# Keys and queries of the next batch loaded half a batch sooner and transposed by DMA in the middle FFN1; first unit with four query tiles and its sampled copies on GpSimd

## The chip, the cores and the metric

The kernel runs on one core of a Trainium2 chip. The metric is the device time of one launch in microseconds (us), the median of several runs; lower is better.

## The reference

Block-sparse attention with 4 batches, 8 heads, 768 tokens, head size 64, followed by a feed-forward network over 3072 tokens of width 512 with 2048 hidden units. Tokens are in 24 blocks of 32.

```python
scores = (1.0 / np.sqrt(D)) * np.matmul(q, k.transpose(0, 1, 3, 2))
mask = np.abs(blk_i - blk_j) <= 1
mask = mask | (blk_i == 0) | (blk_j == 0) | (blk_i == n_blocks - 1) | (blk_j == n_blocks - 1)
for qb in range(n_blocks):
    for kb in sampled_blocks[qb]:            # 3 random blocks for each query block
        mask[qb * 32:(qb + 1) * 32, kb * 32:(kb + 1) * 32] = True
scores = np.where(mask, scores, -1e9)
attn = np.exp(scores - scores.max(-1, keepdims=True))
attn = attn / (attn.sum(-1, keepdims=True) + 1e-09)
x = np.matmul(attn, v)                       # heads put side by side: 3072 x 512
h = x @ w_in
out = (0.5 * h * (1.0 + erf(h / sqrt(2)))) @ w_out
```

Query blocks 0 and 23 see all keys (the dense blocks). Every other block sees 8 blocks: the first, its own three, three sampled ones and the last.

## The kernel before

**Units.** The work is cut into nine units, each some quads (four query blocks, 128 tokens) of one batch: unit 0 is quad 1 of batch 0 and that batch's dense blocks; unit 1 quads 0 and 2; unit 2 quads 3 to 5; then for each of batches 1 to 3 a unit with quads 0 to 2 and the dense blocks (units 3, 5, 7) and one with quads 3 to 5 (units 4, 6, 8). The program alternates: FFN1 of unit n (eight steps of two hidden tiles, `ffn1_step`, Gelu on ScalarE into `g`), then the attention of unit n+1 with FFN2 of unit n (`ffn2_pieces`) filled in between in the amounts of a list of quotas, written by hand.

**Attention.** A unit is a list of rounds: `d` rounds for the dense blocks (one end `x`, one head group `G`), `s` rounds for two sparse blocks. Iteration `it` issues the scores of round it+1 (PE, `sc`), the division of a finished group (`den`, `rec`, `xh` on VectorE), the 32x32 transposes of round it-1 (`pT` or `ptd`, VectorE), the maxima of round it+1 (`nm`, VectorE), the exponentials of round it (`pp`, ScalarE), then hooks, the FFN2 fill, and the values of a group that is complete (`av`, PE). There is one buffer of `av` (psV) and two of scores (psA). Every engine works through its own queue in the program's order.

**Gathered keys and values.** `gb` holds for each sparse query block its eight key blocks. `gather_fixed` (lines 249 to 256, VectorE) copies the blocks whose place is known; `gather` (line 265) copies the sampled ones, one copy for each, at a block number that `block_numbers` has loaded into registers of VectorE or of GpSimd (POOL). For the second unit and part of the third, GpSimd makes the sampled copies.

**Batch 0.** Keys and queries come in with heads side by side (`load_kq`), PE transposes them (`turn_heads`) and ScalarE puts them in place (`place_heads`), keys in `k0`, which lies in the space of `qT1`; line 614 later copies `k0` whole to `kvs[0]`. The value loads (`load_v`, eight) and then the weights (`load_w_in`, `load_w_out`, four each) are issued from GpSimd's queue.

**Batches 1 to 3.** `load_by_token` loads keys and queries in six parts each (line 111, GpSimd's queue), held back by `hold_loads`, a one-element copy that waits for a slice of `g`. `turn` (lines 117 and 118) transposes both by DMA on SP's queue, keys into the space of `ptd`. `place_keys` (line 122, VectorE) scales the keys into `kvs`. Before, the loads for batch b+1 stand in FFN1 of the middle unit (1, 3, 5), `turn` at hook 2 of the attention of units 2, 4 and 6, `place_keys` at the start of the FFN1 of units 2, 4 and 6, just ahead of the gathers, and the value loads there too (batch 1: in FFN1 of unit 0).

Of the kernel before, what the change touches and what calls it, by code (L numbers as in the profile page):

```python
# [19 lines left out]
def kernel(  # L20
# [99 lines left out]
    def place_keys(b):  # L120
        for pr in range(NPR):
            nc.vector.tensor_scalar_mul(
                keys(b)[:, 0:NB, BL * pr:BL * pr + BL].rearrange("p (c n) k -> p c n k", c=NC),
                kTd.rearrange("p (c r n k) -> p r c n k", c=NC, r=NPR, k=BL)[:, pr], 1.0 / 8.0)

# [94 lines left out]
    def place_heads(which, pr, pt):  # L220
        if which == "k":
            nc.scalar.mul(k0[:, 0:NB, BL * pr:BL * pr + BL].rearrange("q n (a i) -> q n a i", i=PI),
                          pt.rearrange("q i (n a) -> q n a i", n=NB), 1.0 / 8.0)
        else:
            nc.scalar.copy(qT0[:, :, pr, :].rearrange("q c (p i) -> q c p i", i=PI),
                           pt.rearrange("q i (c p) -> q c p i", c=NC))

    def spaces():

        views = [psT.tile([P, PI, PP], BF16, name="pt", tag="T")]  # L230
        two = psV.tile([P, 2, 1024], BF16, name="pq", tag="V")
        views += [two[:, i, 0:S].rearrange("p (i c) -> p i c", i=PI) for i in range(2)]
        return views + [psO.tile([P, PI, PP], BF16, name="pt", tag="op")]
# [35 lines left out]
    class Unit:  # L269
        def __init__(self, b, quads, dense, i0=0):  # L270
# [4 lines left out]
            self.rounds = [("d", x, G) for x in (0, 1) for G in (0, 1)] if dense else []  # L275
# [288 lines left out]
    first = [psA.tile([P, 2, 1024], BF16, name="pk", tag="A") for _ in range(2)]  # L564
    first = [x[:, i, 0:S].rearrange("p (i c) -> p i c", i=PI) for x in first for i in range(2)]
    first += spaces()
    for i, (which, pr) in enumerate([(w, pr) for w in "kq" for pr in range(NPR)]):
        turn_heads(which, pr, first[i])
        place_heads(which, pr, first[i])
    spare_key(k0)  # L570
    gather(units[0], units[0].js, known, 0, KC)
    gather_fixed(k0, units[0].place)
    for part in range(4):
        load_w_in(part)
    for part in range(4):
        load_w_out(part)
    others = block_numbers(J0[7:], POOL)
    gather(units[1], J0[7:], others, 0, KC, nc.gpsimd)

    def second_values():  # L580

        nc.gpsimd.tensor_copy(mark, sampled(units[0].place[units[0].js[-1]], NR - 1)[0:1, BW - 1:BW])
        gather(units[1], J0[7:], others, KC, BW, nc.gpsimd)
        ones(1)
    attention(units[0], iter(()), [0] * 7, (0, 0, 0), 5,
              {4: [lambda: gather(units[0], units[0].js, known, KC, BW)], 5: [second_values]})

    QUOTAS = {0: ([4, 3, 1, 1, 0], (1, 2, 1)), 1: ([6, 5, 5, 3, 3, 1, 1], (2, 2, 1))}
    for n, unit in enumerate(units):
# [17 lines left out]
        for s in range(KOUT // 2):  # L607
            ffn1_step(n, 2 * s)
            if s == 0:
                if n == 0:  # L610
                    hold_loads(0)
                    for h in range(H):
                        load_v(1, h)
                    nc.gpsimd.tensor_copy(kvs[0][:, :, 0:KC], k0)
                    gather(units[2], J1[7:], block_numbers(J1[7:], POOL), engine=nc.gpsimd)
                if n > 0 and not fresh and b + 1 < B:
                    hold_loads(0)
                    load_by_token(kn, k, b + 1)
                    load_by_token(qn, q, b + 1)
                if fresh and b + 2 < B:  # L620
                    hold_loads(0)
                    for h in range(H):
                        load_v(b + 2, h)
                if fresh:
                    others = block_numbers(J0[7:], DVE)
            if s == 7 and nxt is not None:
                table(AF.Exp)
            if fresh and s == 0:
                place_keys(b + 1)
                spare_key(keys(b + 1))  # L630
# [6 lines left out]
        elif n in QUOTAS:  # L637
            attention(nxt, filler, *QUOTAS[n],
                      hooks={2: [lambda: turn(1)]} if n == 1 else None)
        elif fresh:  # L640
            attention(nxt, filler, [6, 6, 4, 0, 6, 6, 4, 0, 2, 2, 1], (2, 3, 3), late=True)
        else:
            attention(nxt, filler, [8, 8, 5, 5, 6, 2, 1], (2, 3, 5),
                      hooks={2: [lambda: turn(b + 1)]} if b + 1 < B else None)
# [30 lines left out]
```

## Time and profile before

| | |
|---|---|
| median of 3 runs | 319.88 us (319.59 to 321.11) |
| the profiled execution | 320.74 us, its span 319.0 us |
| mean granted TensorE clock | 0.979 |
| busy, of the span | PE 268.3 us (84%), DVE 218.5 (68%), ACT 208.4 (65%), POOL 88.7 (28%) |
| FFN1 of units 0, 1 and 2 start at | 33.88, 56.52 and 84.48 us |
| FFN1 of units 3 to 8 start at | 122.36, 155.71, 192.99, 225.41, 262.75 and 293.98 us |

Times in the views count from the span's start. In lines of the timeline and of the chain the first two numbers are start and duration in us; then come the engine, the line of the kernel, the operation, what it writes and what it reads, how many, and in brackets the idle time ahead of it with what ended it. "issue" there is time in which the engine waited for nothing that the profile shows. PEld is TensorE's weight load, SPq the issuing queue of SyncE. In the view by stages each row has the stage, its length, and busy time and number of instructions for each engine, then the granted clock, the DMA share and GB/s.

### The profile page before, as it was taken

How to read it: one execution, taken by the hardware profiler on the slowest of the kernel's cores; microseconds unless marked ns; L12 is line 12 of the kernel's file. 1: busy time of each engine (PE TensorE's matmuls, PEld its weight loads, DVE VectorE, ACT ScalarE, POOL GpSimd, SP SyncE). 2: the span in 40 equal slices, each digit the busy share in tenths (PEclk: the TensorE clock that was granted, in tenths of full speed). 3: DMA queues.
4: the chain of work that ended last, by engine and by line, in shares of the span. 5: the costliest groups of instructions: out<-in, count | busy, mean ns of one | idle time of the engine just before them, and what ended most of it. 6: DMA issues, size and time to landing. Idle time of an engine off the chain costs nothing.

```text
span 319.0 us, 12127 instructions
## 1 busy us (share of the span) xinstructions
PE 268.3 (84%) x5240; PEld 147.7 (46%) x5240; DVE 218.5 (68%) x550; ACT 208.4 (65%) x374; POOL 88.7 (28%) x147
## 2 busy tenths in 40 slices
PE   1656877988898879997998889997998789989995
PEld 0615734744453445544553445444543446444643
DVE  6487774798698768785698768874968967673000
ACT  9665483597568775785568765785577765885621
POOL 8659757570070003920160004910000000000000
PEclk9999987799999999998999999999999999999999
DMA  7999999599499100999097101998000000010001
GB/s 110 146 115 208 207 120 31 64 151 171 117 82 52 38 4 35 107 171 189 36 87 47 36 5 37 127 180 159 36 3 35 35 4 35 1 70 4 33 35 67
DMA packets 90632, 25.43 MB, mean 80 GB/s; under 512 B 81745, under 2 KB 87634, under 8 KB 90578
## 3 DMA queue, kind: packets, MB, share of 16 engines
q0 software_dynamic: 68352, 13.64, 79.4%
q1 hardware_dynamic: 22226, 11.01, 14.7%
q8 instruction: 41, 0.67, 0.9%
q14 instruction: 13, 0.11, 0.1%
HBM read 27.26 MB, written 6.29 MB: 105 GB/s over the span
## 4 chain that ended last, share of the span: by engine, by line
PE 66%; DVE 16%; ACT 7%; DMA 5%; issue 3%; POOL 1%; DVEq 0%; POOLq 0%; ACTq 0%
PE hp L451 28%; PE op L470 18%; PE av L403 10%; DVE xh L422 5%; DVE pT L355 4%; PE sc L301 4%; ACT pp L338 4%; DMA w_in_sb<-in_moe_w_in_dram 3%; DVE nm L326 2%; DMA kv<-in_v_dram 2%; PE av L491 2%; PE op L491 2%; DVE rec L420 2%; PE av L379 2%; ACT xT L437 2%
## 5 line engine op out<-in xcount | busy, mean ns | idle before, releaser
L338 ACT ACTIVATE pp<-sc,nm 128x256 bf16<-128x256 f32 (+1 forms) x192 | 92.0, 594 | 22.0 <-DVE nm L326 17.7
L470 PE MATMUL op<-w_out_sb,g 128*128 128x512 bf16 x336 | 91.4, 387 | 2.3 <-ACT os L459 1.3
L451 PE MATMUL hp<-xT,w_in_sb 128*128 128x384 bf16 (+2 forms) x576 | 88.9, 320 | 3.7 <-ACT xT L437 3.7
L454 ACT ACTIVATE g<-hp 128x768 bf16<-128x768 f32 (+4 forms) x81 | 53.8, 676 | 39.2 <-PE hp L451 39.1
L451 PEld LDWEIGHTS <-w_in_sb 128*128 128x128 bf16 x576 | 57.1, 104 | 35.9 <-issue 6.3
L326 DVE TENSOR_REDUCE nm<-sc 128x4 f32<-128x1024 f32 (+1 forms) x48 | 53.4, 1113 | 7.9 <-PE sc L301 7.4
L265 DVE COPY gb<-kv 128x388 bf16 (+1 forms) x240 | 52.2, 295 | 6.1 <-issue 5.9
L403 PE MATMUL av<-kv,pT 64*32 64x130 bf16 x1760 | 39.9, 231 | 15.7 <-DVE xh L422 8.7
L403 PEld LDWEIGHTS <-pT 64*32 64x32 bf16 x2816 | 30.2, 95 | 39.5 <-DVE xh L422 16.4
L470 PEld LDWEIGHTS <-g 128*128 128x128 bf16 x336 | 27.8, 98 | 34.2 <-issue 12.8
L355 DVE STREAM_TRANSPOSE pT<-pp 128x512 f32<-128x512 f32 (+1 forms) x48 | 31.5, 655 | 7.3 <-ACT pp L338 6.9
L147 POOL COPY mark<-g 1x1 bf16<-1x1 bf16 x6 | 6.0, 1002 | 106.6 <-ACT g L454 106.6
L437 ACT COPY xT<-tx 128x512 bf16<-128x512 bf16 (+1 forms) x24 | 13.2, 551 | 28.1 <-PE tx L432 28.1
L301 PE MATMUL sc<-gb,qT 64*32 64x256 bf16 x704 | 19.7, 279 | 10.1 <-ACT pp L338 9.9
L418 DVE TENSOR_SCALAR den<-av 128x8 f32<-128x8 f32 (+2 forms) x28 | 4.5, 161 | 33.9 <-PE av L403 32.2
L130 POOL DMA_DIRECT2D kv<-in_v_dram x32 | 23.3, 735 | 5.2 <-DMA w_out_sb<-in_moe_w_out_dram 3.8
L301 PEld LDWEIGHTS <-qT 64*32 64x32 bf16 x832 | 10.0, 90 | 30.7 <-issue 23.7
L365 ACT ACT_TABLE_LOAD x17 | 21.8, 1283 | 0.3
L403 PE MATMUL av<-gb,pT 64*32 64x130 bf16 x1056 | 20.9, 234 | 0.9 <-issue 0.9
L329 DVE TENSOR_REDUCE nm<-sc 128x1 f32<-128x768 f32 x16 | 15.3, 955 | 6.0 <-PE sc L301 5.5
L422 DVE TENSOR_TENSOR xh<-av,rec 128x512 bf16<-128x512 f32 (+2 forms) x28 | 18.2, 652 | 1.0
L459 ACT COPY os<-op 128x512 f32<-128x512 f32 (+1 forms) x23 | 13.3, 577 | 6.2 <-PE op L491 4.0
(62 smaller groups left out, 203.5 us busy)
## 6 DMA issues: line engine op xcount, KB each, us to landing
out_dram<-os SPq DMA_DIRECT2D x23, 256.0 KB, 2.1
kv<-in_v_dram POOLq DMA_DIRECT2D x32, 96.0 KB, 8.2
kn<-in_k_dram POOLq DMA_DIRECT2D x18, 128.0 KB, 4.6
qn<-in_q_dram POOLq DMA_DIRECT2D x18, 128.0 KB, 5.3
w_in_sb<-in_moe_w_in_dram POOLq DMA_DIRECT2D x4, 512.0 KB, 12.1
w_out_sb<-in_moe_w_out_dram POOLq DMA_DIRECT2D x4, 512.0 KB, 17.6
kn<-in_k_dram POOLq DMA_DIRECT2D x2, 384.0 KB, 5.6
qn<-in_q_dram POOLq DMA_DIRECT2D x2, 384.0 KB, 7.0
```

The lines of the kernel that those rows point to most:

```text
L130: nc.gpsimd.dma_start(out=kvs[b % 2][32 * hh:32 * hh + 32, 0:NB, c0:c0 + D], in_=v[b, h].rearrange("(n p) d -> p n d", p=BL))
L265: (engine or nc.vector).tensor_copy(sampled(unit.place[j], r)[:, None, c0:c1], src[:, bass.ds(at[j][r], 1), :])
L301: nc.tensor.matmul(o, lhsT=qT[rows, j // 4, pr, BL * (j % 4):BL * (j % 4) + BL], rhs=rhs(rows, pr), start=True, stop=True)
L326: nc.vector.tensor_reduce(out=nm[:, 0:2 * n].rearrange("p (g j) -> p g j", g=2), in_=A4[:, :, 0:n, :], op=ALU.max, axis=AX.X, negate=True)
L338: nc.scalar.activation(dst.rearrange("p (c k e) -> p c e k", e=2, k=BL), src.rearrange("p (c e k) -> p c e k", e=2, k=BL), AF.Exp, bias=bias)
L355: nc.vector.transpose(pt[:, 0:w].bitcast(F32), pp[:, 0:w].bitcast(F32))
L365: nc.scalar.activation(junk, zero[0:1, 0:1], func)
L403: nc.tensor.matmul(av[32 * s:32 * s + 32, h, V2 * G:V2 * G + V2], lhsT=pv[rows, c // 2, :, c % 2], rhs=src[rows], start=(c == 0), stop=(c ...
L422: nc.vector.tensor_tensor(xh[rows, :, 0:m * D].rearrange("p h (x d) -> p h x d", d=D), a[:, :, :, 0:D], rec[rows, :, 0:m, None].to_broadca ...
L451: nc.tensor.matmul(hp[:, i, 0:T], lhsT=w_in_sb[:, ki, (m + i) * P:(m + i + 1) * P], rhs=xTs[n % 2][:, ki, 0:T], start=(ki == 0), stop=(ki ...
L454: nc.scalar.activation(g[:, m + i[0]:m + i[1], 0:T], hp[:, i[0]:i[1], 0:T], AF.Gelu)
L470: nc.tensor.matmul(op, lhsT=g[:, m, t * P:(t + 1) * P], rhs=w_out_sb[:, m, :], start=(m == 0), stop=(m == KOUT - 1))
```

## The change

- Batch 0's first unit: keys are turned in the order of four half tiles, so that neighbours are in different tiles, and placed by ScalarE and VectorE in turn; the four query parts have four separate tiles. The fixed key copies come before the queries. The sampled copies of unit 0 move from VectorE to GpSimd, keys ahead of the weight loads, values (after the hook of iteration 4) between the second and the third load of `w_out`; then follow the last two `w_out` loads and unit 1's sampled copies.
- Dense rounds are ordered with the head group outside.
- In FFN1 of unit 0 GpSimd copies `k0` to `kvs[0]`, loads keys and queries of batch 1 (no more the values), makes unit 2's sampled copies and sets the ones.
- In FFN1 of units 1, 3 and 5: `turn` and the value loads of the next batch. `place_keys`, now with `spare_key` in it, goes to hook 3 of the attention of units 2, 4 and 6.
- Keys and queries of batches 2 and 3 are loaded in FFN1 of units 2 and 4, from its fourth step on.

```diff
@@ -122,6 +122,7 @@
             nc.vector.tensor_scalar_mul(
                 keys(b)[:, 0:NB, BL * pr:BL * pr + BL].rearrange("p (c n) k -> p c n k", c=NC),
                 kTd.rearrange("p (c r n k) -> p r c n k", c=NC, r=NPR, k=BL)[:, pr], 1.0 / 8.0)
+        spare_key(keys(b))
 
     def load_v(b, h):
         G, hh = divmod(h, 4)
@@ -217,20 +218,17 @@
                                     src[0:PP, 2 * pr + h2, i * D:(i + 1) * D],
                                     identity[0:PP, 0:PP])
 
-    def place_heads(which, pr, pt):
+    def place_heads(which, pr, pt, on_act):
         if which == "k":
-            nc.scalar.mul(k0[:, 0:NB, BL * pr:BL * pr + BL].rearrange("q n (a i) -> q n a i", i=PI),
-                          pt.rearrange("q i (n a) -> q n a i", n=NB), 1.0 / 8.0)
+            dst = k0[:, 0:NB, BL * pr:BL * pr + BL].rearrange("q n (a i) -> q n a i", i=PI)
+            seen = pt.rearrange("q i (n a) -> q n a i", n=NB)
+            if on_act:
+                nc.scalar.mul(dst, seen, 1.0 / 8.0)
+            else:
+                nc.vector.tensor_scalar_mul(dst, seen, 1.0 / 8.0)
         else:
             nc.scalar.copy(qT0[:, :, pr, :].rearrange("q c (p i) -> q c p i", i=PI),
                            pt.rearrange("q i (c p) -> q c p i", c=NC))
-
-    def spaces():
-
-        views = [psT.tile([P, PI, PP], BF16, name="pt", tag="T")]
-        two = psV.tile([P, 2, 1024], BF16, name="pq", tag="V")
-        views += [two[:, i, 0:S].rearrange("p (i c) -> p i c", i=PI) for i in range(2)]
-        return views + [psO.tile([P, PI, PP], BF16, name="pt", tag="op")]
 
     def spare_key(kT):
         nc.vector.tensor_copy(kT[:, NB, :], kT[:, 0, :])
@@ -272,7 +270,7 @@
             self.groups = [[j for j in range(4 * t, 4 * t + 4) if 0 < j < NB - 1] for t in quads]
             self.js = [j for grp in self.groups for j in grp]
             self.place = {j: i for i, j in enumerate(self.js, i0)}
-            self.rounds = [("d", x, G) for x in (0, 1) for G in (0, 1)] if dense else []
+            self.rounds = [("d", x, G) for G in (0, 1) for x in (0, 1)] if dense else []
             self.ends = {3: tuple(self.rounds)} if dense else {}
             for grp in self.groups:
                 r = [("s", tuple(grp[i:i + 2])) for i in range(0, len(grp), 2)]
@@ -561,29 +559,37 @@
     J0, J1 = units[3].js, units[2].js
     value_list()
     known = block_numbers(units[0].js, DVE)
-    first = [psA.tile([P, 2, 1024], BF16, name="pk", tag="A") for _ in range(2)]
-    first = [x[:, i, 0:S].rearrange("p (i c) -> p i c", i=PI) for x in first for i in range(2)]
-    first += spaces()
-    for i, (which, pr) in enumerate([(w, pr) for w in "kq" for pr in range(NPR)]):
-        turn_heads(which, pr, first[i])
-        place_heads(which, pr, first[i])
+    pairs = [psA.tile([P, 2, 1024], BF16, name="pk", tag="A") for _ in range(2)]
+    pairs.append(psV.tile([P, 2, 1024], BF16, name="pq", tag="V"))
+    pairs = [[x[:, i, 0:S].rearrange("p (i c) -> p i c", i=PI) for i in range(2)] for x in pairs]
+    first = {("k", pr): pairs[pr % 2][pr // 2] for pr in range(NPR)}
+    first |= {("q", 0): psT.tile([P, PI, PP], BF16, name="pt", tag="T"), ("q", 1): pairs[2][0],
+              ("q", 2): psO.tile([P, PI, PP], BF16, name="pt", tag="op")}
+
+    def first_heads(which, prs):
+        for pr in prs:
+            turn_heads(which, pr, first[which, pr])
+            place_heads(which, pr, first[which, pr], which == "q" or pr % 2)
+    first_heads("k", range(NPR))
     spare_key(k0)
-    gather(units[0], units[0].js, known, 0, KC)
     gather_fixed(k0, units[0].place)
+    first["q", 3] = psA.tile([P, PI, PP], BF16, name="pt", tag="A")
+    first_heads("q", range(NPR))
+    first_known = block_numbers(units[0].js, POOL)
+    gather(units[0], units[0].js, first_known, 0, KC, nc.gpsimd)
     for part in range(4):
         load_w_in(part)
-    for part in range(4):
+    for part in range(2):
         load_w_out(part)
     others = block_numbers(J0[7:], POOL)
-    gather(units[1], J0[7:], others, 0, KC, nc.gpsimd)
-
-    def second_values():
-
-        nc.gpsimd.tensor_copy(mark, sampled(units[0].place[units[0].js[-1]], NR - 1)[0:1, BW - 1:BW])
+
+    def sampled_values():
+        gather(units[0], units[0].js, first_known, KC, BW, nc.gpsimd)
+        for part in range(2, 4):
+            load_w_out(part)
+        gather(units[1], J0[7:], others, 0, KC, nc.gpsimd)
         gather(units[1], J0[7:], others, KC, BW, nc.gpsimd)
-        ones(1)
-    attention(units[0], iter(()), [0] * 7, (0, 0, 0), 5,
-              {4: [lambda: gather(units[0], units[0].js, known, KC, BW)], 5: [second_values]})
+    attention(units[0], iter(()), [0] * 7, (0, 0, 0), 5, {4: [sampled_values]})
 
     QUOTAS = {0: ([4, 3, 1, 1, 0], (1, 2, 1)), 1: ([6, 5, 5, 3, 3, 1, 1], (2, 2, 1))}
     for n, unit in enumerate(units):
@@ -609,25 +615,25 @@
             if s == 0:
                 if n == 0:
                     hold_loads(0)
-                    for h in range(H):
-                        load_v(1, h)
                     nc.gpsimd.tensor_copy(kvs[0][:, :, 0:KC], k0)
+                    load_by_token(kn, k, 1)
+                    load_by_token(qn, q, 1)
                     gather(units[2], J1[7:], block_numbers(J1[7:], POOL), engine=nc.gpsimd)
+                    ones(1)
                 if n > 0 and not fresh and b + 1 < B:
-                    hold_loads(0)
-                    load_by_token(kn, k, b + 1)
-                    load_by_token(qn, q, b + 1)
-                if fresh and b + 2 < B:
+                    turn(b + 1)
                     hold_loads(0)
                     for h in range(H):
-                        load_v(b + 2, h)
+                        load_v(b + 1, h)
                 if fresh:
                     others = block_numbers(J0[7:], DVE)
+            if s == 3 and fresh and b + 2 < B:
+                hold_loads(6)
+                load_by_token(kn, k, b + 2)
+                load_by_token(qn, q, b + 2)
             if s == 7 and nxt is not None:
                 table(AF.Exp)
             if fresh and s == 0:
-                place_keys(b + 1)
-                spare_key(keys(b + 1))
                 gather_fixed(keys(b + 1), nxt.place)
                 gather(nxt, J0[:7], known)
                 gather(nxt, J0[7:], others)
@@ -636,12 +642,12 @@
             last_output(n)
         elif n in QUOTAS:
             attention(nxt, filler, *QUOTAS[n],
-                      hooks={2: [lambda: turn(1)]} if n == 1 else None)
+                      hooks={3: [lambda: place_keys(1)]} if n == 1 else None)
         elif fresh:
             attention(nxt, filler, [6, 6, 4, 0, 6, 6, 4, 0, 2, 2, 1], (2, 3, 3), late=True)
         else:
             attention(nxt, filler, [8, 8, 5, 5, 6, 2, 1], (2, 3, 5),
-                      hooks={2: [lambda: turn(b + 1)]} if b + 1 < B else None)
+                      hooks={3: [lambda: place_keys(b + 1)]} if b + 1 < B else None)
 
 
 # ---- launch: one core; inputs and outputs as the reference has them ----
```

## The prediction

> **What bounds the kernel.** I read the page's chain first, then the timeline of the first 70 us, then the same stages of different batches against each other, then the DMA landings.
>
> ```profile
> PE 66%; DVE 16%; ACT 7%; DMA 5%; issue 3%; POOL 1%; DVEq 0%; POOLq 0%; ACTq 0%
> ```
>
> PE sets the end; DVE is the next engine on the path, so a DVE step counts where PE waits for it. The chain over the attention of unit 4 (batch 1, DMA transposes in it) and of unit 8 (batch 3, none) is the cleanest evidence:
>
> ```profile
> 144.76 0.69 DVE xh L422
> 145.45 0.63 DVE pT L355
> 146.12 0.55 PE av L403 x41
> 146.66 0.94 issue
> ...
> 155.71 10.56 PE hp L451 x64
> ...
> 217.64 0.91 issue
> ...
> 225.41 10.56 PE hp L451 x64
> ...
> 286.38 0.70 PE av L403 x60
> ...
> 293.98 10.56 PE hp L451 x64
> ```
>
> Counted from their FFN1 starts (122.36, 192.99, 262.75), units 4, 6 and 8 reach this `av` after 23.76, 23.63 and 23.63 us: equal. They reach the next FFN1 after 33.35, 32.42 and 31.23. So what the transposes (SP, 138.6 to 148.3 and 209.2 to 219.1) take along costs 2.12 us in unit 4 and 1.19 in unit 6, beginning with an "issue" gap of 0.9. Unit 4 also has a half-clock spell right behind it (clock 0.68 in 147 to 151). The 10.56 us of FFN1 are the same with 12 loads beside it, with 8 and with none.
>
> The first unit, and the two engines whose copies will meet:
>
> ```profile
> 24.92 2.51 DVE L265 COPY gb<-kv 128x260 bf16 x12
> 25.36 2.93 POOL L265 COPY gb<-qT 128x128 bf16 x12 [0.56 <-DVE nm L326]
> ...
> 28.36 4.14 POOL L265 COPY gb<-kv 128x260 bf16 x12
> ...
> 32.46 1.80 DVE L249 COPY gb<-qT 128x768 bf16<-128x768 bf16 x6
> ...
> 37.21 1.33 DVE L265 COPY gb<-qT 128x128 bf16 x9 [1.77 <-issue]
> ...
> 38.46 1.66 DVE L265 COPY gb<-kv 128x260 bf16 x9
> ```
>
> ```profile
> 124.80 2.33 POOL L147 COPY mark<-g 1x1 bf16<-1x1 bf16 x1 [31.35 <-ACT g L454]
> ```
>
> ```profile
> 24.90:25.36 0.46, 0.44 (x4) 0.00 (x0) 1.00 1.21 203
> 25.36:27.30 1.94, 1.94 (x10) 1.94 (x9) 1.00 1.25 207
> ```
>
> The last fence is L265 by stage (DVE, then POOL): DVE begins 4 copies in 0.46 us alone, but 10 in 1.94 us (0.19 each) beside POOL's 9. And POOL's one-element `mark` copy, 0.18 us when alone, takes 2.33 while DVE copies without a pause. SBUF copies of these two engines hold each other up.
>
> **First unit.** Keys placed by ACT and DVE in turn, query tiles that don't wait for one another, and 12 key copies (1.58 us) gone from DVE bring `nm` forward by 0.5 to 1 us. A DVE copy of a 128x768 PSUM tile isn't in the trace; between 0.29 (L122, from SBUF) and 0.96 (L329, from PSUM) I take 0.9, and either way it is covered, because the next gate is a DMA: the eighth value load, issued at 12.46, lands 11.3 us later by the DMA view, at 23.8, and the dense `av` (L379, 23.94 to 26.82) needs it. That stays. Then, with no 2.51 us gather in DVE's queue: den, rec, xh take 0.8 us (to 27.65), `pT` 0.7 (28.35); POOL's value copies start at 23.8 and take 12 x 0.345 = 4.14 (28.0). Sparse `av` resumes at 28.35 and not 29.43: 1.08 us won. POOL's 12 key copies ahead of the weight loads move the first w_in issue from 14.31 to about 17.5, still behind the value loads' landing; w_in's last part, needed 4.8 us into FFN1 (37.6), landed at 33.1: cost nothing, and if the loads slid by more than 4 us, that excess. The last two w_out parts, issued at 28 and not 22.8, queue behind the earlier ones (landing till 38.2) and are first needed after 43: nothing.
>
> **Unit 1's copies: the largest term.** What POOL did in 24 to 36 it now does from 28.0: two w_out issues (1.5), 12 key copies (0.24 each), 12 value copies (0.345 each), then at once, no longer after eight loads at 45.11, the whole-key copy:
>
> ```profile
> 45.11 2.86 POOL L614 COPY kv<-qT 128x3200 bf16<-128x3200 bf16 x1
> ```
>
> DVE at the same time (from 31.4, FFN1 starting at 32.8) has its fixed copies (3 us), the register load (1.77) and 18 sampled copies, and `nm` and Exp of unit 1 queue behind. Lower bound, no interference: all as before and 1.08 earlier, Exp at 41.06. Upper bound, POOL standing while DVE's fixed copies run, as `mark` did: POOL has 8 key copies done by 31.4, goes on at 34.4, ends its values at 39.5 and L614 at 42.5; DVE starts sampled copies at 36.1, gets 10 done at POOL's 0.345, waits out L614, does the last 8 at 0.17: 43.9, Exp at 44.9 (nm takes 0.95), 2.8 late against 42.14. If POOL isn't held during the fixed copies, its values end at 36.6, L614 at 39.7, DVE at 42.4, Exp at 43.4: 1.3 late. Only the question whether DVE waits for a long POOL copy to its end has no row; the nearest are POOL's wait for DVE and DVE's slower pace beside short ones, both of which say it waits. I take the middle of 1.3 and 2.8: **+2.1**, with the 1.08 already in it; bounds -1.1 to +2.8. The Trainium skill, page "SBUF — State Buffer", section "Who interferes with whom", says that whichever of a DVE two-port copy and a GpSimd instruction issues first makes the other block fully until it is done; the 2.33 us `mark` agrees, and by the rule alone this term would be at its upper end, 322.6 in all.
>
> **FFN1 of unit 1.** POOL's twelve key/query loads (0.89 each, from about 41) run to 52, its register load (2.7 at worst), 12 copies (5.51) and ones (1.44) to 60 or later, so they now meet DVE's fixed and sampled copies (55.1 to 65.9 before). DVE was just late there already: `nm` at 65.82 behind the last copy, scores done at 65.52. Five fixed copies each behind a 0.46 us POOL copy are +2.3 at most, 0 at least; I take **+0.4**, since most of POOL's copies fall before. Value loads behind `turn` end by 70 and are needed at 84; `turn` is issued on SP behind one store and ahead of none until 70.6, and its wait for the query loads (landing by about 58) holds nobody before the key placing at 75: nothing.
>
> **Key placing in attention (units 2, 4, 6).** Four copies (1.17) and spare (0.19), 1.37 us with gaps, now stand in DVE's queue behind `nm` of round 4, and den, xh, `pT`, `nm` 5 queue behind them, with PE's next `av` waiting for xh:
>
> ```profile
> 73.52 1.19 DVE L326 TENSOR_REDUCE nm<-sc 128x4 f32<-128x1024 f32 x1
> ...
> 74.79 0.17 DVE L418 TENSOR_SCALAR den<-av 128x8 f32<-128x8 f32 x1
> ```
>
> Unit 2 has no gap there (74.71 to 74.79): +1.3. Units 4 and 6 have 0.99 and 0.86 of idle: +0.5 each (0 to 1.4). What leaves FFN1 of units 2, 4 and 6 is worth nothing: after the gathers `nm` waits 0.17 for PE's scores there, and 1.94 in unit 6. Batches 2 and 3: loads held until step 6 of FFN1 find POOL without other work and have some 25 us to land; the new order of dense rounds changes no operation. Nothing.
>
> **Transposes out of attention.** Unit 4 -2.1, unit 6 -1.2, unit 2 -0.3 (its issue gap of 0.26). In FFN1 they lie beside 64 long matmuls, and no row shows transposes there: nothing (bounds 0 and 0.9, one issue gap, each).
>
> **Sum.** The profiled execution took 320.74 (span 319.0), 0.86 above the median of 319.88, about what unit 4's half-clock spell adds over unit 6; that is in a term here, so I start from 320.74. +2.1 +0.4 +1.0 (unit 2: 1.3 - 0.3) -1.6 (unit 4) -0.7 (unit 6) = +1.2: **321.9 us**.
>
> **Rivals.** (A) The engines hardly collide, not slower: L614 and POOL's copies leave DVE its 0.15 to 0.18 per copy, or POOL is through before DVE starts its sampled copies. Then the term is -1.08 and FFN1's is 0: 320.74 - 1.08 + 1.0 - 1.6 - 0.7 = 318.4. It decides if DVE ends unit 1's copies before 39.6. Against it: ten copies in 1.94 us. For it: DVE is held only where POOL is copying, and POOL may be earlier or later than I think. (B) The issue gaps move and aren't removed: transposes reach into the first third of the attention of units 2, 4 and 6 (second one landing some 14 to 16 us after the FFN1 start, which takes 10.56), and the loads of batches 2 and 3 into the dense attention of units 3 and 5. 0.9 in each of the first three takes back what units 4 and 6 give: 321.9 + 2.7 = 324.6. It decides if an issue gap lies in those stretches; against it, the loads until 140 cost unit 4 nothing. (C) The clock: it was halved around 46 to 49 and 53 to 60, and FFN1 of unit 1 took 8.6 where two thirds of 10.56 would be 7.0. Without these spells 1.6 us or more is won, 320.3 or below; more idle PE at 41 to 44 speaks against.
>
> **Numbers.** Main case 0.52, own range 320.3 to 323.4 (term bounds 1.3 and 2.8, and 0.5 either way on the rest); A 0.28 (317.4 to 319.6); B 0.13; C 0.07. 0.5% is 1.6 us, about what a measurement tells from no change: faster is below 318.3, slower above 321.5. Slower: 0.33 of the main case and all of B, 0.47 with a rest from C; faster: half of A and half of C, 0.20; same: 0.33. The range 317.9 to 324.8 leaves out the ends of A and B.
>
> **What would show it.** L614 soon after 36, with a DVE copy of L265 standing behind it; first Exp of unit 1 at 43.4 or later (41.1 would be A); sparse `av` of unit 0 at about 28.4; no issue gap in units 4 and 6 behind their fourth round; `den` behind L122 in units 2, 4, 6. Wrong if the sampled copies run at 0.15 to 0.18 throughout, or the issue gaps turn up elsewhere.

## The result and the profile after

| | before | after |
|---|---|---|
| median, same chip | 320.50 us (319.59 to 322.14, 4 runs) | 335.08 us (332.93 to 337.13, 4 runs) |
| ratio to before | 1 | 1.0448, 95% interval 1.0366 to 1.0531 |
| the profiled execution, its span | 320.74, 319.0 | 337.13, 335.1 |
| mean granted TensorE clock | 0.979 | 0.964 |

The change makes the kernel 4.5% slower: 14.6 us, where the prediction had 1.2. The direction is the one forecast; the size is not, and 335.08 lies far outside 317.9 to 324.8. The profiled execution of the changed kernel is the slowest of its four, so its span differs by more than the medians do: 16.1 us.

Where it goes is seen from the starts of the nine FFN1 stages (the `hp` matmuls of 64, from the timeline of PE), us:

| FFN1 of unit | 0 | 1 | 2 | 3 | 4 | 5 | 6 | 7 | 8 |
|---|---|---|---|---|---|---|---|---|---|
| before | 33.88 | 56.52 | 84.48 | 122.36 | 155.71 | 192.99 | 225.41 | 262.75 | 293.98 |
| after | 33.58 | 56.76 | 93.00 | 131.25 | 168.78 | 206.22 | 241.47 | 278.76 | 310.07 |
| change of the distance | -0.30 | +0.54 | **+8.28** | +0.37 | **+4.18** | +0.16 | **+2.83** | -0.05 | +0.08 |

Of the 16.1 us of span, 15.3 are in three stretches: FFN1 of the middle unit (1, 3, 5) and the attention behind it. These are the stages that have `turn` and the value loads in the changed kernel. The new order of dense rounds and the loads in FFN1 of units 2 and 4 (distances +0.37 and +0.16) cost next to nothing in this execution.

Such distances come from one execution each. In two kernels that are unchanged behind units 3 and 5 (the first half of experiment 5 and experiment 8 below) they are 32.75 and 31.34 us, and 32.79 and 31.59, where the kernel before has 33.35 and 32.42. Differences of about 1 us there say little. The granted clock differs as well: over the stretches behind units 1, 3 and 5 it is 0.94, 0.95 and 1.00 before, and 0.86, 0.95 and 0.95 after. How much of the 8.28 and 2.83 us lies in these spells of lower clock, and not in the waits told below, no experiment separates.

The page of the changed kernel, shares of the chain by engine:

```profile
PE 44%; DVE 23%; issue 11%; DMA 7%; POOL 6%; ACT 5%; DVEq 2%; POOLq 1%; ACTq 0%
```

PE has gone from 66% to 44%. "issue" (3% before) and DVE (16%) have most of what PE lost, and POOL, with 1% before, stands on the path with 6%. The chain itself, over FFN1 of unit 3 and the attention of unit 4 (columns: start, us, what):

```profile
135.46 0.51 DVE gb L263 x3
135.97 6.34 issue
...
144.03 0.89 issue
...
154.46 2.00 issue
...
158.00 1.08 DVE kv L122 x4
...
168.78 10.56 PE hp L449 x64
```

Before, PE's FFN1 lay on the chain here, with the gathers hidden beside it. Now the gathers are the chain, and 6.34 us of it are "issue" on DVE: no work, no semaphore. In the view of DVE's waits (us in total, times, longest) the gathers' "issue" time was 7.7 us before, at most 1.8 at a time. Now it is:

```profile
DVE gb L263 <- issue: 22.6, 9, 6.5
...
DVE gb L247 <- POOL gb L263: 4.5, 1, 4.5
...
DVE gb L254 <- POOL gb L263: 0.9, 1, 0.9
```

What DVE's queue does in the time ahead of the sampled copies is in the list of the instructions of one line. It is the load of block numbers into DVE's registers (line 206; 205 before), which is not counted as busy (ns: least, median, most):

```profile
L205 DVEq TENSOR_LOAD <-vf x13: 753/1404/2127, 7.1 to 269.5; - x13
```

```profile
L206 DVEq TENSOR_LOAD <-vf x13: 742/1403/7599, 7.1 to 285.5; - x13
```

The median is the same, the longest has gone from 2.13 to 7.60 us. DVE and SP side by side, in FFN1 of unit 3 of the changed kernel:

```profile
132.40 3.69 SPq L117 DMA_TRANSPOSE ptd<-kn  x1
136.31 5.20 SPq L118 DMA_TRANSPOSE qT<-qn  x1
```

```profile
142.41 1.62 DVE L263 COPY gb<-kv 128x388 bf16 x9 [6.44 <-issue]
145.02 1.11 DVE L263 COPY gb<-kv 128x388 bf16 x6 [0.99 <-issue]
```

The load (135.08 to 142.23 in the trace) begins while SP is issuing the transposes and ends 0.7 us after SP is through (141.51). The 0.99 us ahead of the last six copies is the next load, which SP no longer disturbs.

The first stretch has something else besides, and it begins in FFN1 of unit 0. POOL:

```profile
32.61 4.33 POOL L263 COPY gb<-kv 128x260 bf16 x12
...
42.30 2.85 POOL L618 COPY kv<-qT 128x3200 bf16<-128x3200 bf16 x1 [5.11 <-DVE gb L263]
...
50.31 5.30 POOL L111 DMA_DIRECT2D qn<-in_q_dram  x6
57.36 6.48 POOL L263 COPY gb<-kv 128x388 bf16 x12 [1.76 <-issue]
```

and DVE:

```profile
33.85 2.69 DVE L252 COPY gb<-qT 128x1152 bf16<-128x1152 bf16 x1
...
60.16 2.27 DVE L247 COPY gb<-kv 128x1536 bf16<-128x1536 bf16 x3 [4.54 <-POOL gb L263]
...
68.24 4.58 DVE L263 COPY gb<-kv 128x388 bf16 x21 [3.73 <-issue]
```

POOL's whole-key copy (L618) waits 5.11 us for DVE's gathers; twelve loads and a register load follow; unit 2's sampled copies, which ended at 53.55 before, end at 63.84; and DVE's fixed copies stand 4.54 and 0.85 us for them. Then comes a register load of 4.16 us beside the transposes (1.91 before). DVE is through its sampled copies at 72.82 and not at 65.89; the first Exp of unit 2 is at 73.99 and not at 67.29.

### The profile page after: what moved, and what is told of

Read it like the earlier page. It is cut to its first block, busy times and chain, and to the rows that moved or that the text cites. A ratio compares the mean times of both kernels' runs of the same rounds, so it can differ in the third digit from the quotient of the medians.

```text
span 335.1 us, 12061 instructions
## 1 busy us (share of the span) xinstructions
PE 260.8 (78%) x5175; PEld 145.3 (43%) x5240; DVE 210.5 (63%) x528; ACT 207.2 (62%) x372; POOL 97.8 (29%) x170
## 4 chain that ended last, share of the span: by engine, by line
PE 44%; DVE 23%; issue 11%; DMA 7%; POOL 6%; ACT 5%; DVEq 2%; POOLq 1%; ACTq 0%
PE hp L449 16%; PE op L468 13%; PE av L401 7%; DVE xh L420 4%; DVE nm L324 4%; DMA w_out_sb<-in_moe_w_out_dram 4%; DVE gb L263 4%; PE sc L299 3%; DMA kv<-in_v_dram 3%; ACT pp L336 3%; DVE pT L353 3%; POOL gb L263 2%; DVEq L206 2%; PE av L489 2%; POOL kn L111 2%
## 5 line engine op out<-in xcount | busy, mean ns | idle before, releaser
L449 PE MATMUL hp<-xT,w_in_sb 128*128 128x384 bf16 (+2 forms) x576 | 86.3, 312 | 4.0 <-ACT xT L435 3.9
L468 PE MATMUL op<-w_out_sb,g 128*128 128x512 bf16 x272 | 79.4, 399 | 7.4 <-issue 5.7
L449 PEld LDWEIGHTS <-w_in_sb 128*128 128x128 bf16 x576 | 55.0, 100 | 35.4 <-issue 6.3
L263 DVE COPY gb<-kv 128x388 bf16 (+1 forms) x228 | 40.8, 257 | 21.2 <-issue 20.7
L299 PE MATMUL sc<-gb,qT 64*32 64x256 bf16 x704 | 21.8, 301 | 24.7 <-ACT pp L336 14.3
L148 POOL COPY mark<-g 1x1 bf16<-1x1 bf16 x6 | 8.0, 1335 | 105.4 <-ACT g L452 105.4
L327 DVE TENSOR_REDUCE nm<-sc 128x1 f32<-128x768 f32 x16 | 15.3, 955 | 13.9 <-PE sc L299 13.5
```

Source lines behind the costliest of these rows:

```text
L263: (engine or nc.vector).tensor_copy(sampled(unit.place[j], r)[:, None, c0:c1], src[:, bass.ds(at[j][r], 1), :])
L299: nc.tensor.matmul(o, lhsT=qT[rows, j // 4, pr, BL * (j % 4):BL * (j % 4) + BL], rhs=rhs(rows, pr), start=True, stop=True)
L449: nc.tensor.matmul(hp[:, i, 0:T], lhsT=w_in_sb[:, ki, (m + i) * P:(m + i + 1) * P], rhs=xTs[n % 2][:, ki, 0:T], start=(ki == 0), stop=(ki ...
L468: nc.tensor.matmul(op, lhsT=g[:, m, t * P:(t + 1) * P], rhs=w_out_sb[:, m, :], start=(m == 0), stop=(m == KOUT - 1))
```

## The theories

**T**: DVE's load of block numbers stands still while SP issues the transposes of `turn`, and this carries the loss behind units 3 and 5 and part of that behind unit 1. **V**: it is the value loads, issued from POOL in the same stage, that hold DVE up. **The POOL theory**: in FFN1 of unit 1 the late sampled copies are the larger part. Against all of them, **the first unit** (tiles, POOL's copies of unit 0) might have put the engines out of step. Ratios below are to the kernel before on the same chip, with their 95% intervals; runs without a ratio were one execution.

## The experiments

**1. The transposes alone, added to the kernel before** (FFN1 of unit 7, where nothing else is new; results not used):

```diff
             if s == 0:
...
+                if n == 7:
+                    turn(b + 1)
```

> The kernel before, with one thing added: two DMA transposes on SP's queue in the FFN1 of unit 7 (where no loads run), into space that nothing reads any more. Theory T (a register load of VectorE, the instruction that brings block numbers from SBUF into registers, stands still while SP issues DMA transposes): the 2.06 us register load of that FFN1 takes 5 to 8 us and ends within 1 us of SP's last issue, the first maxima of unit 8 come about 3 us later than 273.7, and the time is 2.5 to 4 us longer than before. Rival V (the value loads on GpSimd's queue hold the register load, and the transposes only happen to be there): the register load stays at 2.1 us and the time within 0.7 us of before.

Measured: 320.58 us, kernel before 320.57. The first load in this FFN1 took 5.17 us instead of 2.06, and DVE resumed as SP ended (270.48):

```profile
262.49 4.34 SPq L117 DMA_TRANSPOSE ptd<-kn  x1
266.88 3.60 SPq L118 DMA_TRANSPOSE qT<-qn  x1
```

```profile
270.36 1.62 DVE L265 COPY gb<-kv 128x388 bf16 x9 [4.12 <-issue]
```

So two transposes are enough to hold the load, without value loads or early loads. The time expected for the end was too long: the next FFN1 started only 0.7 us late. DVE was 1.3 us ahead of PE here, and the load was 3.1 longer, not 5.

**2. The changed kernel with transposes and key placing back in their old places**, the value loads left where the change put them:

```diff
                 if n > 0 and not fresh and b + 1 < B:
-                    turn(b + 1)
                     hold_loads(0)
...
             if fresh and s == 0:
+                place_keys(b + 1)
                 gather_fixed(keys(b + 1), nxt.place)
...
-                      hooks={3: [lambda: place_keys(1)]} if n == 1 else None)
+                      hooks={2: [lambda: turn(1)]} if n == 1 else None)
...
-                      hooks={3: [lambda: place_keys(b + 1)]} if b + 1 < B else None)
+                      hooks={2: [lambda: turn(b + 1)]} if b + 1 < B else None)
```

> The changed kernel with the transposes put back to hook 2 of the attention and the key placing back to the start of FFN1; the value loads stay in the FFN1 of units 1, 3 and 5. T: the register loads in the FFN1 of units 3 and 5 go from 7.2 and 7.6 us back to 2.1, the one of unit 1 from 4.2 to about 2, and the time falls from 335 to 323 to 327 us, what is left being unit 1's late start behind GpSimd. V: the register loads stay long beside the value loads, 333 to 336 us.

Measured: 327.07 us (326.83 to 331.0), ratio 1.024 (1.0142 to 1.0338): 8.0 us of the 14.6 are back. The key placing's share is among them. The longest load is 2.08 us again, with POOL issuing the value loads beside it:

```profile
L206 DVEq TENSOR_LOAD <-vf x13: 741/1439/2079, 7.1 to 275.3; - x13
```

The distances behind units 3 and 5 are 32.91 and 31.64 us, no longer than before. T holds against V. What stays is the stretch behind unit 1 (33.21, before 27.96), where DVE still waits for POOL:

```profile
59.64 2.27 DVE L247 COPY gb<-kv 128x1536 bf16<-128x1536 bf16 x3 [4.65 <-POOL gb L263]
```

**3. The transposes held until DVE's last gather is through** (one element of `ptd` written by DVE ahead of them):

```diff
+                    nc.vector.tensor_copy(kTd[0:1, 0:1], zero[0:1, 0:1])
                     turn(b + 1)
```

> The changed kernel, in which the transposes of each FFN1 also wait for VectorE's last gather of that FFN1 (a one-element write of VectorE into the space that they overwrite); all else in place. T: the register loads are back at 2.1 us with the value loads still beside them, units 4 and 6 start their maxima as in the kernel before, and the time is 324 to 328 us; transposes now lie in the attention again, with issue gaps of about 1 us there. V: register loads stay at 6 to 7 us and the time at 333 us or more.

Measured: 330.83 us (329.43 to 333.05), ratio 1.0332 (1.0241 to 1.0423). The loads take 2.1 us, as T has it, but the transposes now lie in the attention and beside the value loads, where the first of them took 7.91 us to issue, and PE has "issue" gaps of 1.23 and 0.53 us there. This run parts the load from the rest of the stage: the value loads, the transposes and the key placing all stay in the stretches behind units 3 and 5, only the transposes come later, and these take 34.23 and 31.98 us instead of 37.53 and 35.25 (33.35 and 32.42 before). So up to 3.3 us of the loss in each go with the load; the granted clock over both is 1.00 here and 0.95 in the changed kernel. The stretch behind unit 1 stays at 35.96 us (36.24 in the changed kernel, 27.96 before), though its register load is at 1.58 us. That is why the time is above the 324 to 328 expected.

**4. POOL's order**: unit 2's sampled copies and the ones ahead of the twelve loads.

```diff
-                    load_by_token(kn, k, 1)
-                    load_by_token(qn, q, 1)
                     gather(units[2], J1[7:], block_numbers(J1[7:], POOL), engine=nc.gpsimd)
                     ones(1)
+                    load_by_token(kn, k, 1)
+                    load_by_token(qn, q, 1)
```

> The changed kernel with one reordering on GpSimd's queue in FFN1 of unit 0: unit 2's twelve sampled copies and the ones come ahead of the twelve key and query loads of batch 1 and not behind them. Theory O (in FFN1 of unit 1 VectorE's fixed copies wait until GpSimd's late sampled copies are through, 4.5 and 0.9 us, and then run into the transposes): no such waits, the first Exp of unit 2 at 66 to 69 and not 74.0 us, and 327 to 330 us in all. Rival (unit 1 is late because of the transposes alone, 2 us of register load): 332 us or more.

Measured: 339.03 us (336.73 to 340.82), ratio 1.0591 (1.0502 to 1.068). DVE no longer waits for POOL, and the first Exp of unit 2 is at 67.23, as before the change; yet FFN1 of unit 2 starts at 93.03, no sooner. The loads and so the transposes are later and now meet the value loads, and the key placing waits for them:

```profile
69.47 10.87 SPq L118 DMA_TRANSPOSE qT<-qn  x1
```

```profile
78.46 1.17 DVE L122 TENSOR_SCALAR kv<-ptd 128x768 bf16<-128x768 bf16 x4 [2.99 <-DMA ptd<-kn]
```

The local gain of 6.8 us was given back whole one stage later: the batch's loads, transposes and placing are themselves a chain, and here it had no slack once it began late.

**5. and 6. The two halves of the change alone**: the first unit (tiles, placing, POOL's sampled copies) without the rest, and the rest without the first unit.

> The kernel before with the changes of the first unit alone (key and query tiles, placing by two engines, order of dense rounds, sampled copies of unit 0 on GpSimd with the weight loads around them); loads, transposes and key placing where they were. Theory R (the rest of the change, above all the transposes beside VectorE's register loads and GpSimd's late copies in FFN1 of unit 1, costs the time): 319 to 321.5 us, FFN1 of unit 1 starting within 0.5 us of 56.5 and no wait of VectorE's fixed copies for GpSimd there. Rival F (the collision of copies in FFN1 of unit 0, the largest term of the prediction): 322 us or more.

> The other half: the first unit as before, with the loads half a batch sooner, the transposes in FFN1 of the middle units beside the value loads, and the key placing at hook 3. R: register loads of 4 to 8 us in the FFN1 of units 1, 3 and 5 and 331 to 336 us. F: 326 us or less.

Measured: the first unit alone 320.61 us, ratio 1.0045 (1.0018 to 1.0071); the rest alone 334.96 us, ratio 1.0471 (1.0428 to 1.0514), with loads of 4.15, 7.20 and 7.27 us in FFN1 of units 1, 3 and 5. The loss is the rest's; the first unit costs about 1.4 us.

**7. Edits 2 and 4 together.**

> The changed kernel with the transposes and the key placing back (as in the run of that name) and GpSimd's queue in unit 0's FFN1 reordered (sampled copies of unit 2 ahead of the loads). If GpSimd's late copies are what the first left, FFN1 of unit 2 starts at 84 to 86 us and not 89.3, and the time is 321 to 324 us; if not, it stays at 326 to 328.

Measured: 324.62 us (320.89 to 325.82), ratio 1.0134 (1.01 to 1.0168). First Exp of unit 2 at 66.39 and the distances behind units 3 and 5 (32.04 and 31.22) are as expected, but FFN1 of unit 2 starts at 90.09, not at 84 to 86: the transposes lie at 72 to 83 in the attention, beside late loads, and PE stands still for 3.19 us in the middle of a group of `av`:

```profile
80.33 0.40 PE L401 MATMUL av<-kv,pT 64*32 64x130 bf16 x10 [3.19 <-issue]
```

So the stretch behind unit 1 takes 34.71 us (27.96 before) with neither the wait for POOL nor the long register load in it. The granted clock over it is 0.85 (0.94 before). Transposes beside late loads, gaps of PE and a lower clock stand there together, and which of them carries these 6.8 us is open: batch 1's new order of loads was not run with all else as before.

**8. Only the tiles and the placing of the first unit, and the order of the dense rounds**, in the kernel before.

> The kernel before with only the tiles and the placing of the first unit (keys placed by two engines, four query tiles, dense rounds by head group); the sampled copies stay on VectorE and nothing moves on GpSimd's queue. If the gate of the first unit is the eighth value load (landing at 23.9), VectorE's value copies follow at once and end at about 26.4, FFN1 of unit 0 starts 0.5 to 1 us sooner than at 33.9, no copies collide, and the time is 318.5 to 320 us against about 320.5 for the kernel before. Rival: the value copies were the gate themselves and start when they did, no change within 0.5 us.

Measured: 320.04 us, ratio 1.0000 (0.9971 to 1.0028). So the 0.45% of experiment 5 come with what was moved on POOL's queue (the sampled copies and the weight loads around them), not with the tiles. The local expectation failed: FFN1 of unit 0 started at 35.42 us, 1.5 later than in the kernel before and not 0.5 to 1 sooner.

**9. and 10. Batches 2 and 3 alone, in the kernel before**: first only the new order of loads (keys and queries in FFN1 of units 2 and 4, values in that of units 3 and 5), then `turn` and `place_keys` moved as well (the lines that move `place_keys` to hook 3 are left out here).

```diff
-                if n > 0 and not fresh and b + 1 < B:
+                if n == 1:
                     hold_loads(0)
-                    load_by_token(kn, k, b + 1)
-                    load_by_token(qn, q, b + 1)
-                if fresh and b + 2 < B:
+                    load_by_token(kn, k, 1)
+                    load_by_token(qn, q, 1)
+                elif n > 0 and not fresh and b + 1 < B:
+                    turn(b + 1)            # second kernel only
                     hold_loads(0)
                     for h in range(H):
-                        load_v(b + 2, h)
+                        load_v(b + 1, h)
...
+            if s == 3 and fresh and b + 2 < B:
+                hold_loads(6)
+                load_by_token(kn, k, b + 2)
+                load_by_token(qn, q, b + 2)
```

> The kernel before, in which batches 2 and 3 alone get the new order of loads (keys and queries in the FFN1 of units 2 and 4, values in the FFN1 of units 3 and 5); the transposes stay at hook 2 of the attention of units 4 and 6, key placing stays in FFN1, and batch 1 and the first unit are as before. Theory T (the transposes beside VectorE's register load carry the loss of batches 2 and 3, and the early loads carry none): register loads in the FFN1 of units 3 and 5 stay at 2.1 us, the stages from the FFN1 of unit 3 to 4 and of unit 5 to 6 are 32.9 and 31.6 as in the kernel with the turn back (33.35 and 32.42 before), so 319.3 beside a kernel before of 320.5, ratio 0.994 to 1.000. Theory V (the early order itself costs): 2 us or more in those stages or in the stage from unit 2 to 3 (39.65 with the turn back, 37.88 before), 322 or above.

> The same, and for batches 2 and 3 the two transposes go to the FFN1 of units 3 and 5 and key placing to hook 3 of the attention of units 4 and 6, as in the changed kernel; batch 1 and the first unit are as before. Theory T: register loads in the FFN1 of units 3 and 5 take 7.0 to 7.7 us, the two stages are 37.5 and 35.2 us, and the time is 7.0 above the kernel before, 327.5; what is left of the changed kernel's loss (about 8) belongs to batch 1. Theory Q (the late batches lose only because batch 1 has put the engines out of step): the stages stay within 1.5 us of before, 320 to 323.

Measured: the order of loads alone 320.67 us, ratio 1.0028 (0.9995 to 1.0062), with 33.03 and 31.49 us behind units 3 and 5: neither a loss nor the gain that those two stages promised. With `turn` moved 330.55 us, ratio 1.0312 (1.027 to 1.0354), where T had 327.5: loads of 7.25 and 7.08 us, as T has it, so the late batches lose by themselves. But the distances are not those expected: 33.47 and 38.09 behind units 3 and 5, and 41.46 between FFN1 of units 2 and 3 (37.88 before, 37.85 in experiment 9, which has the same work there). PE stood 1.80 us at 116.69 and 2.83 us at 222.41 for "issue", and the granted clock over the two long stretches was 0.92 and 0.91 (1.00 in experiment 9 and before). So the load's length came as T has it, and the place of the loss did not; that a late DVE costs less where PE is late itself would fit, and is not shown. The share of batch 1 can't be read off by subtraction (14.6 less these 10.2): putting `turn` and the key placing of all batches back gained 8.0 us (2), less than moving those of the late batches alone costs, so the parts don't add up.

**11. Is it SP's queue?** Experiment 1 with the two transposes issued from ScalarE's queue. **12. Is it transposes?** Experiment 1 with four plain SBUF copies of the same buffers in runs of 64 elements, on SP's queue. Both edits in one cut; in 11 `turn` takes its queue as an argument.

```diff
-                    turn(b + 1)                        # experiment 1
+                    turn(b + 1, nc.scalar)             # 11: the queue that issues
+                    copy_by_head()                     # 12: in its place
...
+    def copy_by_head():
+        for dst, src in ((kTd, kn), (qTs[0].rearrange("p c r s -> p (c r s)"), qn)):
+            to, of = (x.rearrange("p (n j d) -> p j n d", j=2, d=D) for x in (dst, by_token(src)))
+            for j in range(2):
+                nc.sync.dma_start(out=to[:, j], in_=of[:, 1 - j])
```

> The kernel before with the two transposes once more in the FFN1 of unit 7 (their results are not used), issued from ScalarE's queue instead of SyncE's. Theory T in its general form (VectorE's register load stands until an issue of transposes is over, whatever queue issues them): the load takes 4.5 to 6 us again, as in the run with SyncE issuing (5.17 beside 2.06 before). Theory S (it is SyncE's queue that the load waits for): 2.1 us. ScalarE is blocked for about 8 us in this FFN1, so its Gelu and PE come late, 323 to 329; that part says nothing.

> The kernel before with four plain SBUF copies by DMA on SyncE's queue in the FFN1 of unit 7, of the same two buffers in runs of 64 elements, in the place of the two extra transposes (results not used). Theory T (the issue of a transpose is what holds the load): the load stays at 2.1 us. Theory Q (any long issue on SyncE's queue, or many small descriptors, holds it): 3 us or more. Time within 0.5 us of the kernel before.

Measured, 11: 332.59 us, kernel before 320.41; the load took 6.74 us and ended 0.6 us after ACT's issue (274.19), so it isn't SP's queue alone. The end is later than the 323 to 329 expected; PE waited 6.43 us for Gelu behind the issue. 12: 324.02 us, kernel before 320.41, where the expectation had 0.5 us between them; the next FFN1 started 2.8 us late. The two loads of this FFN1 took 4.66 and 4.17 us instead of 2.06 and 1.40:

```profile
263.96 4.40 SPq L124 DMA_DIRECT2D ptd<-kn  x2
268.41 5.62 SPq L124 DMA_DIRECT2D qT<-qn  x2
```

```profile
271.32 1.62 DVE L271 COPY gb<-kv 128x388 bf16 x9 [3.60 <-issue]
276.70 1.33 DVE L271 COPY gb<-kv 128x388 bf16 x6 [3.75 <-issue]
```

So T falls in its narrow form: plain copies cut into small runs hold the load too. And "until the issue is over" holds, within 2 us, for transposes only: here the first load ended (271.14) 2.9 us before SP was through (274.03), and the second stayed slow 2.5 us past it. All loads that began beside such an issue, with what was left of it then:

| run, FFN1 of unit | issue left, us | load, us | undisturbed, us |
|---|---|---|---|
| after, 1 | 3.1 | 4.16 | 1.91 |
| after, 3 | 6.4 | 7.16 | 2.07 |
| after, 5 | 7.2 | 7.60 | 2.06 |
| transposes only (1), 7 | 5.5 | 5.17 | 2.06 |
| POOL's order (4), 1, 3 and 5 | 17.6, 6.4, 7.9 | 0.75, 7.37, 7.05 | 0.75, 2.07, 2.06 |
| second half alone (6), 1, 3 and 5 | 2.2, 6.8, 6.5 | 4.15, 7.20, 7.27 | 1.91, 2.07, 2.06 |
| late batches turned (10), 3 and 5 | 8.2, 6.6 | 7.25, 7.08 | 2.07, 2.06 |
| ScalarE issues (11), 7 | 6.1 | 6.74 | 2.06 |
| plain copies (12), 7 | 7.5, then 1.7 | 4.66, then 4.17 | 2.06, 1.40 |

One load wasn't held at all: the 0.75 us of experiment 4, which began at 62.70, 0.06 us after the first transpose's issue had begun (62.64), and was over 5.8 us before that issue was.

The Trainium skill, page "Perfetto Trace Analysis", section "DMA Instruction — HWDGE (DVE, Sync)", says that one block makes the descriptors of the hardware DMAs, that DVE's and SP's sequencers share it, and that it is locked for one of them until all descriptors of an instruction are made. The transposes agree with that in the main (the held loads took 4.15 to 7.60 us and ended between 0.9 us before and 1.9 us after the issue), experiment 12 does not quite, and that a register load passes through this block no run shows. Why the load stands is therefore open; that it does, and for how long, is shown.

Loading all of DVE's registers before `turn` is issued was not tried. None of the twelve kernels beat the kernel before.

## Why the prediction was wrong, step by step

- **"In FFN1 they lie beside 64 long matmuls, and no row shows transposes there: nothing (bounds 0 and 0.9, one issue gap, each)": this step failed.** It looked for the cost on PE and priced it with PE's issue gaps. The cost is on DVE: register loads 5.1, 5.5 and 2.2 us longer in units 3, 5 and 1. The load stood in the trace of before as an idle time of DVE ("1.00 <-issue") ahead of each group of gathers, and in the page's chain as DVEq with 0%; the prediction named it among DVE's work and never asked what else could hold it. For the same reason "holds nobody" was wrong for `turn`: DVE stands while it is issued, without waiting for its semaphore. Experiments 1 and 11 show the held load by itself; experiment 3 bounds what it costs, up to 3.3 us of the loss behind unit 3 and as much behind unit 5.
- **"Unit 4 -2.1, unit 6 -1.2" with the key placing: -1.6 and -0.7 expected, +4.18 and +2.83 measured**, 5.8 and 3.5 off. The added load times (5.1, 5.5) are most of it in unit 4 and more than all in unit 6. The gain of taking the transposes out of the attention came whole in unit 6 only (first `nm` to the next FFN1 20.27 us, 21.44 before); in unit 4 the query transposes landed 18.0 us after their issue beside the value loads, and a gap of 2.00 us stands at 154.46, twice that of before. So rival B was partly right: a gap moved. The gain itself was mis-sized for unit 6: in experiment 8 and the first half of experiment 5, with the transposes in the attention as before, unit 6 takes 31.59 and 31.34 us, 0.1 to 0.4 more than unit 8's 31.23, so most of the 1.19 that the prediction put on the transposes was that execution's.
- **"FFN1 of unit 1 ... I take +0.4, since most of POOL's copies fall before": failed.** POOL's loads were to run from about 41 to 52; they ran from 45.09 to 55.6, because L618 waited 5.11 us for DVE. So the sampled copies lay at 57.36 to 63.84, in front of DVE's fixed copies, which waited 5.4 us for them. That they wait by semaphore is what the trace says; why fixed copies depend on these sampled ones was not tried. The upper bound of 2.3 counted pushes of 0.46 us and not a wait for the group. With the 2.2 us of the register load this makes 7.6 us at the first Exp of unit 2, of which 6.7 show (73.99 against 67.29). But that this is also what the kernel lost there is not shown: with the wait and the held load gone (7), the attention behind took the time instead, and why stays open.
- **"Unit 1's copies: the largest term", +2.1: mis-sized.** The local forecast was good (first Exp 43.44, forecast 43.4 to 44.9; the fixed copy L252 took 2.69 us beside POOL's copies, 0.56 before), but FFN1 of unit 1 started only 0.24 us late, because the attention took 1.06 us less; why is open. L618 was in nobody's way, since it came after DVE's gathers. The Trainium skill, page "SBUF — State Buffer", section "Who interferes with whom", has a DVE copy in two-port mode and a GpSimd instruction exclude each other until the first is done; that the copies hold each other up agrees, and the 2.13 us that L252 took longer are six of POOL's 0.36 us copies, not one.
- **Key placing: right.** PE's wait for `xh` grew by 1.44 us in unit 2 (expected 1.3) and by 0.57 in unit 6 (0.5). `den` stands behind L122, as foreseen:

```profile
81.36 1.15 DVE L122 TENSOR_SCALAR kv<-ptd 128x768 bf16<-128x768 bf16 x4
...
82.65 0.16 DVE L416 TENSOR_SCALAR den<-av 128x8 f32<-128x8 f32 x1
```

- **First unit: right up to the last step.** Sparse `av` resumed at 28.29 (28.35 forecast), but a 0.58 us issue gap of PE at 29.34 left 0.30 of the 1.08 us for FFN1.
- **Rivals.** A (hardly a collision) is excluded by its own sign: DVE ended unit 1's copies at 42.17 us, not before 39.6. C (the clock gains) went the other way: 0.964, not above 0.979. None of the three names the register load.

The sum by its own terms: 1.9 too much at unit 1, and 6.9, 5.8 and 3.5 too little behind units 1, 3 and 5; that is 14.3 of the 14.9 us between 1.2 forecast and 16.1 found in the span. That the direction came out right was luck: the term that gave it, +2.1, measured 0.24, and the loss came from a step put at nothing and one put at 0.4.

## What to carry to other kernels

Before a DMA transpose, or a DMA copy in short runs, is moved beside an engine's work, look at the instructions that the profile doesn't count as busy: the register loads of the engine that gathers by index, and the "issue" time ahead of the copies. A transfer that nobody waits for can still hold an engine up: here the register loads stood about as long as the issue of the transposes lasted, from SP's queue and from ScalarE's. And where the moved step is one of a chain (load, transpose, place, gather), a gain at one link is worth nothing until the links behind it have been dated too: experiments 3, 4 and 7 each mended one wait and met the next.

## What the runs showed that was not expected

**PE's "issue" gaps end shortly after a packet of instructions has landed.** The trace has the packets of an instruction queue, 16,384 bytes each. In the traces of the fourteen kernels PE has 61 issue gaps of 0.35 us or more from 29 us on, and each ends 1.2 to 2.1 us after such a packet has landed (most 1.3 to 1.5). Most packets take 0.9 to 1.4 us; those ahead of the nine gaps of 2 us or more took 1.7 to 2.5, with one exception, beside other loads or transposes: 152.17 to 154.55 ahead of the 2.00 us gap of the changed kernel, 221.76 to 223.80 ahead of the 2.83 in experiment 10 (the exception is the 3.19 of experiment 7, with a packet of 1.15 that only began at 77.79, when PE already stood). That the gaps are waits for PE's own instructions is the likely reading, though the packets don't name their engine; that traffic delays them is what their place suggests. No run isolates either. The Trainium skill, page "Runtime: NRT & Kernel Launch", section "Instruction fetch mechanics", has instructions come in blocks of 16 KiB, as here, and calls the cost of a boundary mostly hidden: most of the 41 packets of an execution have no such gap behind them (37 of 41 in the kernel before), and all 61 gaps lie in the attention.

**The issue of the same transpose took 3.6 to 10.9 us** (3.60 in experiment 1, 10.87 in experiment 4), and in FFN1 of units 3 and 5 of the changed kernel the query transpose landed 18.0 and 16.7 us after issue, beside the value loads, against 7.3 to 7.7 in the kernel before. DVE's register loads stayed at 2.08 and 1.49 us with the value loads beside them in experiment 2 (2.06 and 1.40 undisturbed). Beside POOL's key and query loads in FFN1 of unit 1 they took 2.56 and 2.44 in experiments 4 and 7 (1.91 undisturbed), far less than beside the transposes.
